# A thresholded attention with a leaky MoE layer behind it: the first periods rebuilt, and unread products on TensorE

## The chip, the cores and the metric

The kernel runs on one core of one Trainium2 chip. The metric is device time in microseconds. One core has five engines that run side by side, each through its own list of instructions in order: TensorE (PE in the profile, with its weight loads as PEld), VectorE (DVE), ScalarE (ACT), GpSimd (POOL) and SyncE (SP, which here only issues transfers). An engine waits where an instruction needs something that another engine or a transfer has not finished.

## The reference

```python
def _attn_ref(q, k, v, tau):                  # q, k, v: (8, 8, 576, 64), tau = 0.02
    scale = 1.0 / np.sqrt(q.shape[-1])
    scores = scale * np.matmul(q, k.transpose(0, 1, 3, 2))
    thresh = np.max(scores, axis=-1, keepdims=True) - tau
    scores = np.where(scores >= thresh, scores, -1000000000.0)
    scores = scores - np.max(scores, axis=-1, keepdims=True)
    attn = np.exp(scores)
    attn = attn / (np.sum(attn, axis=-1, keepdims=True) + 1e-09)
    return np.matmul(attn, v)

def _moe_ref(x, w_in, w_out):                 # x: (4608, 512), w_in: (512, 2048), w_out: (2048, 512)
    h = x @ w_in
    g = np.maximum(0.01 * h, h)
    return g @ w_out
# the output is _moe_ref of the attention's output, heads side by side
```

The threshold makes a score's last digits matter: a score just above or just below it is kept or lost. So the kernel computes scores from q and k split into two fp16 halves each (a high one and what is left, a low one), with three products out of the four.

## The kernel before

**Periods.** The attention is cut into 72 periods: 9 for each of the 8 batches. A period has one pair of heads and 256 of the first 512 queries as two chunks of 128 (8 periods: two blocks of queries by four pairs), or the last 64 queries of all eight heads (the ninth, `st.tail`). The main loop over `n` writes out by hand what each engine gets in iteration `n`, and each engine keeps to that order:

- `scores`: 24 matmuls (48 in a tail period) into one PSUM tile `sc` of five banks. Its four regions are (chunk, head). Head 0 and head 1 use different rows of the array, and the list alternates between them. Since regions (1, 0) and (1, 1) share bank 2, head 1's part of it waits for an empty instruction of GpSimd (`signal`, a `nop` at L246) that follows head 0's part.
- `copies`: VectorE copies the four regions to SBUF with the sign turned and the scale applied, taking the row minimum on the way (L257), and works out the threshold `th` (L259).
- `widen(n-1)` and `turn_w(n-1)`: GpSimd spreads the reciprocals of the row sums (L292), and SP issues the transposing transfer `wT <- w` (L297).
- `low_at`, `loads_at`, `turns_at`, `pool_at`: work for coming batches, put down by iteration. GpSimd splits q and k into halves (L144, L150, L154) and casts v (L105, L110); SP loads; TensorE turns the halves (`turn`, L183) and ScalarE copies them out (L186, L190). GpSimd also issues the loads of the MoE weights, `w_in` (L114) and `w_out` (L117), which cast on the way.
- ScalarE: `exp_plain` on three regions (L271), `exp_steep` on the fourth (a steep Prelu at L276 and an exponential at L277).
- MoE: two rounds, each with one unit of `layer1` (16 or 32 matmuls, L349, then L351 on ScalarE) and two units of `layer2` (4 matmuls each, L362), taken from the queues `l1q` and `l2q`. A group of four periods makes 256 tokens and gives 8 units of layer 1 and 16 of layer 2.
- `pv(n-2)`: weights times v (L309), two periods behind (`PV_LAG`), and after it VectorE's `evacuate` (L329, L321), which multiplies by the reciprocal and writes the MoE's input `x`.
- `weights` (L282), three on VectorE, with the row sums, and `finish`: the reciprocal (L288) of the four row sums, which needs ScalarE's steep region too.

PSUM tiles with the tag "h" (turned halves, `pv`, layer 1) share two buffers; layer 2 has one of its own ("o"). Before the loop, the first keys of batch 0 are split and turned: pair 0's k and q, then the k tails, on ScalarE and VectorE (`split_now`, L164 and L165), the others on GpSimd.

Of the kernel before, what the change touches and what calls it, by code (L numbers as in the profile page):

```python
# [9 lines left out]
FP32 = mybir.dt.float32  # L10
FP16 = mybir.dt.float16
# [3 lines left out]
PV_LAG = 2  # L15
# [21 lines left out]
def kernel(  # L37
# [24 lines left out]
    ident = sb.tile([128, 128], FP16, name="ident")  # L62
    minus_tau = sb.tile([128, 1], FP32, name="minus_tau")
# [18 lines left out]
    def load_tails(b, which):  # L82
        t = sb.tile([128, 2, 2, 64], FP32, tag="rawt", bufs=2, name="rawt")
        src = SRC[which][b, :, MAIN:S, :].rearrange("(u sh) p d -> u p sh d", u=2)
        for u in range(2):
            nc.sync.dma_start(out=t[ds(64 * u, 64), :, :, :].rearrange("p s h d -> p (s h) d"), in_=src[u])
        tails[b, which] = t
# [35 lines left out]
    turned, halves, scaled = {}, {}, {}  # L123
# [44 lines left out]
    def turn(key, copy=None):  # L168
        copy = copy or nc.scalar.copy
        b, p, which = key  # L170
        dst, half = turned_of(b, which), halves.pop(key)
        n = 2 if p == "t" else 4
        c0 = 0 if which == "q" else 64
        if p == "t":
            c0 = MAIN if which == "q" else 0
            tp = ps.tile([128, 2, 2, 2, 64], FP16, tag="h", bufs=2, name="tp")
        else:
            tp = ps.tile([128, 2, 4, 128], FP16, tag="h", bufs=2, name="tp")
        for x in range(2):
            for t in range(n):  # L180
                for h in range(2):
                    o = tp[ds(64 * h, 64), x, :, t, :] if p == "t" else tp[ds(64 * h, 64), x, t, :]
                    nc.tensor.transpose(o, half[:, x, t, h, :], ident[:, :])  # L183
        if p == "t":
            for x in range(2):
                copy(out=dst[:, x, :, ds(c0, 64)], in_=tp[:, x, :, :, :].rearrange("d u s p -> d (u s) p"))  # L186
            if which == "k":
                nc.gpsimd.tensor_copy(out=dst[:, :, :, 576:640], in_=dst[:, :, :, 0:64])
        else:
            copy(out=dst[:, :, p, ds(c0, 512)], in_=tp[:, :, :, :].rearrange("d x t p -> d x (t p)"))  # L190
# [38 lines left out]

    def scores(st):  # L230

        (a00, a01), (b01, b00) = pieces(0, 0), pieces(0, 1)
        (a11, a12), (b12, b11) = pieces(1, 0), pieces(1, 1)
        todo = [[(1, a12), (0, a00), (0, a01), (1, a11)], [(0, b00), (0, b01), (1, b11), (1, b12)]]
        todo = [[(c, x, i) for c, x in row for i in range(3)] for row in todo]
        at_, signal = [0, 0], None
        while todo[0] or todo[1]:
            h = 1 if not todo[0] or (todo[1] and at_[1] < at_[0]) else 0
            c, x, i = todo[h].pop(0)
            at_[h] += x[1]  # L240
            for mm in product(st, c, h, x, i):
                if (h, x) == (1, b12) and i == 0:
                    tc.add_manual_dep(mm.ins, signal.ins.name, BEHIND, reason="the row halves share a bank")
                last = mm
            if (h, x) == (0, a12) and i == 2:
                signal = nc.gpsimd.nop()  # L246
                tc.add_manual_dep(signal.ins, last.ins.name, BEHIND, reason="the row halves share a bank")

    TILES = ((0, 1), (0, 0), (1, 0), (1, 1))

    def copies(st):
        st.mn = sb.tile([128, 4], FP32, tag="mn", bufs=2, name="mn")
        st.th = sb.tile([128, 4], FP32, tag="th", bufs=2, name="th")
        st.s = {}
        for n, t in enumerate(TILES):
            st.s[t] = sb.tile([128, 576], FP32, tag=f"s{n}", bufs=1, name="s")
            nc.vector.tensor_scalar(out=st.s[t][:, :], in0=sc[:, ds(PLACE[t], 576)], scalar1=-1.0 / UNIT, scalar2=None,  # L257
                                    op0=AX.mult, op1=AX.min, accum_out=st.mn[:, n : n + 1])
        nc.vector.tensor_scalar(out=st.th[:, :], in0=st.mn[:, :], scalar1=1.0, scalar2=tau_f, op0=AX.mult, op1=AX.add)  # L259
        st.w = sb.tile([128, 2, 10, 128], FP16, tag="w", bufs=3, name="w")  # L260
        st.sum = sb.tile([128, 2, 2], FP32, tag="sum", bufs=3, name="sum")
        st.e = {}
# [23 lines left out]
    def finish(st):  # L286
        rec = sb.tile([128, 2, 2], FP32, tag="rec", bufs=2, name="rec")
        nc.vector.reciprocal(out=rec[:, :, :], in_=st.sum[:, :, :])  # L288
        st.rec = rec
# [24 lines left out]
    def evacuate(st, n):  # L314
# [17 lines left out]
        if done:  # L332
            nu = 8 if xg.tokens == 256 else 4
            l1q.extend((xg, u, nu, n + 1) for u in range(nu))
# [50 lines left out]
    def at(d, n, f):  # L385
        d.setdefault(n, []).append(f)
# [10 lines left out]
    def split_at(n, key):  # L397
        if key[0]:
            at(pool_at, n - 2, lambda key=key: split_scale(key))
            at(pool_at, n - 2, lambda key=key: split_high(key))  # L400
            at(low_at, n - 1, lambda key=key: split_low(key))
        else:
            at(pool_at, n - 1, lambda key=key: split_pool(key))
        at(turns_at, n, lambda key=key: turn(key))

    for b in range(1, B):
        base = PERB * (b - 1)
        for i, (s, w_) in enumerate(((0, "k"), (0, "q"), (1, "k"), (1, "q"))):
            at(loads_at, base + ((-2, -1, 2, 3)[i] if b > 1 else (1, 1, 3, 3)[i]),
               lambda b=b, s=s, w_=w_: load_main(b, s, w_))  # L410
        for i, w_ in enumerate("kq"):
            at(loads_at, base + ((-1, 5)[i] if b > 1 else (2, 4)[i]), lambda b=b, w_=w_: load_tails(b, w_))
        for i, key in enumerate(units(b)):
            split_at(base + 2 + 8 * i // 10 if b > 1 else base + 4 + i // 2, key)
    for b in range(B):
        base = PERB * (b - 1)
        if b:
            for s in range(2):
                at(loads_at, base + 5 + s, lambda b=b, s=s: load_v(b, s))
            at(loads_at, base + 6, lambda b=b: load_vtails(b))  # L420
        for p in range(NP):
            at(pool_at, base + 8 + p if b else 2 + p // 2, lambda b=b, p=p: cast_v(b, p))
        at(pool_at, base + 8 if b else 2, lambda b=b: cast_vtails(b))


    masks.make_identity(nc, ident[:, :])
    nc.gpsimd.memset(minus_tau[:, :], -tau_f)
    load_pair(0, "k", nc.sync)
    load_pair(0, "q", nc.scalar)
    load_tails(0, "k")  # L430
    load_pair(1, "q", nc.scalar)
    load_pair(1, "k", nc.sync)
# [11 lines left out]
    for i in range(4):  # L444
        load_w(i)
        at(pool_at, 3 + i, lambda i=i: load_w(4 + i))

    first = units(0)
    for key in first[:3]:
        split_now(key)  # L450
    turn(first[0])
    turn(first[1], nc.vector.tensor_copy)
    turn(first[2])
    for i, key in enumerate(first[3:]):
        if i < 2:
            split_pool(key)
            at(turns_at, 0, lambda key=key: turn(key))
        else:
            split_at((0, 0, 1, 1, 2, 2, 3)[i], key)
# [3 lines left out]
    while n < N + PV_LAG or l1q or l2q or stores:  # L463
        st = periods[n] if n < N else None
        if st:
            scores(st)
            copies(st)
        if 1 <= n <= N:
            widen(periods[n - 1])
            turn_w(periods[n - 1])  # L470
        for f in low_at.get(n, []):
            f()
        for f in loads_at.get(n, []):
            f()
        while stores:
            store()
        for f in turns_at.get(n, []):
            f()
        for f in pool_at.get(n, []):
            f()  # L480
        if st:
            exp_plain(st, 0)
        for half in range(2):
            if l1q and l1q[0][3] <= n:
                layer1()
            for _ in range(2):
                if l2q:
                    layer2()
            if st:
                if half == 0:  # L490
                    exp_plain(st, 1)
                    exp_plain(st, 2)
                else:
                    exp_steep(st, 3)
        if n >= PV_LAG and n - PV_LAG < N:
            pv(periods[n - PV_LAG])
        if st:
            weights(st, 0)
            weights(st, 1)
        if n >= PV_LAG and n - PV_LAG < N:  # L500
            evacuate(periods[n - PV_LAG], n)
        if st:
            weights(st, 2)
            finish(st)
        n += 1
# [33 lines left out]
```

## Time and profile before

| | us |
|---|---|
| median of 3 runs | 527.36 |
| the runs | 525.57, 527.36, 527.87 |
| the profiled execution's own time | 526.85 |
| its span, first to last instruction | 525.1 |
| PE busy | 472.8 (90%) |
| DVE busy | 435.1 (83%) |
| ACT busy | 422.3 (80%) |
| POOL busy | 256.3 (49%) |

Some 1.75 us of the profiled execution lie outside its span, and it is 0.5 us under the median. The first copy of period 0 starts at 16.04 us of the span, that of period 9 at 86.40, that of period 71, the last one, at 483.34. So the first nine periods take 70.4 us, 7.8 each, and the 62 after them 396.9 us, 6.40 each. What follows period 71 is the rest of the MoE work on TensorE.

### The profile page before, as it was taken

How to read it: one execution, taken by the hardware profiler on the slowest of the kernel's cores; microseconds unless marked ns; L12 is line 12 of the kernel's file. 1: busy time of each engine (PE TensorE's matmuls, PEld its weight loads, DVE VectorE, ACT ScalarE, POOL GpSimd, SP SyncE). 2: the span in 40 equal slices, each digit the busy share in tenths (PEclk: the TensorE clock that was granted, in tenths of full speed). 3: DMA queues.
4: the chain of work that ended last, by engine and by line, in shares of the span. 5: the costliest groups of instructions: out<-in, count | busy, mean ns of one | idle time of the engine just before them, and what ended most of it. 6: DMA issues, size and time to landing. Idle time of an engine off the chain costs nothing. (4 is left out here: it accounts for less than half of the span.)

```text
span 525.1 us, 18850 instructions
## 1 busy us (share of the span) xinstructions
PE 472.8 (90%) x7744; PEld 372.1 (71%) x7744; DVE 435.1 (83%) x1231; ACT 422.3 (80%) x714; POOL 256.3 (49%) x410
## 2 busy tenths in 40 slices
PE   4666768998989999999999999999999999999995
PEld 3444556776777777777777777777777777777783
DVE  1778868999899999999899989999899989999300
ACT  3567678888989998898989998898989998778541
POOL 5889953655375645654384636563385531100000
PEclk9999689999999999999999999999999999999999
DMA  8978999588988699978998699789988796666511
GB/s 204 241 178 175 201 199 209 112 171 195 205 179 183 123 225 227 173 146 203 215 171 176 170 207 215 160 130 225 201 155 202 158 192 144 122 102 151 133 42 61
DMA packets 230806, 90.34 MB, mean 172 GB/s; under 512 B 201024, under 2 KB 227648, under 8 KB 230720
## 3 DMA queue, kind: packets, MB, share of 16 engines
q1 hardware_dynamic: 227488, 84.43, 76.7%
q0 software_dynamic: 2688, 4.19, 4.7%
q8 instruction: 60, 0.98, 0.8%
q10 hardware_dynamic: 544, 0.52, 0.3%
q14 instruction: 26, 0.21, 0.1%
HBM read 36.70 MB, written 9.44 MB: 88 GB/s over the span
## 5 line engine op out<-in xcount | busy, mean ns | idle before, releaser
L257 DVE TENSOR_SCALAR_CACHE_REDUCE s<-sc 128x576 f32<-128x576 f32 x288 | 199.0, 748 | 12.0 <-PE sc L227 11.5
L282 DVE SCALAR_TENSOR_TENSOR w<-s,th,e 128x576 f16<-128x576 f32 x216 | 184.2, 876 | 8.6 <-ACT e L271 1.1
L271 ACT ACTIVATE e<-s,mn 128x576 f16<-128x576 f32 x216 | 158.7, 773 | 20.2 <-DVE s L257 19.2
L362 PE MATMUL o<-wout,g 128*64 128x512 f16 x1152 | 148.9, 380 | 5.0 <-ACT osb L368 3.5
L349 PEld LDWEIGHTS <-win 128*64 128x64 f16 x2560 | 127.4, 110 | 29.2 <-issue 16.0
L349 PE MATMUL hp<-x,win 128*64 128x256 f16 x2048 | 134.4, 273 | 8.4 <-ACT kT L190 4.5
L227 PE MATMUL sc<-kT,qT 64*128 64x256 f16 (+7 forms) x1920 | 128.4, 298 | 12.0 <-DVE s L257 4.7
L292 POOL CAST w<-rec 128x256 f16<-128x256 f32 x72 | 28.7, 399 | 211.8 <-DVE rec L288 199.6
L227 PEld LDWEIGHTS <-qT 64*128 64x128 f16 (+1 forms) x1920 | 97.9, 101 | 35.0 <-issue 19.5
L351 ACT ACTIVATE g<-hp 128x512 f16<-128x512 f32 x144 | 84.6, 588 | 13.0 <-PE hp L349 13.0
L362 PEld LDWEIGHTS <-g 128*64 128x64 f16 x1152 | 69.6, 110 | 35.5 <-issue 8.5
L154 POOL TENSOR_TENSOR half<-scaled,half 128x512 f16<-128x512 f32 (+1 forms) x77 | 82.5, 1079 | 0.6
L309 PE MATMUL pv<-wT,v 128*64 128x256 f16 (+1 forms) x960 | 55.6, 251 | 12.2 <-DMA wT<-w 6.7
L309 PEld LDWEIGHTS <-v 128*64 128x64 f16 x960 | 44.6, 112 | 25.9 <-POOL v L105 5.3
L277 ACT ACTIVATE w<-s,minus_tau 128x576 f16<-128x576 f32 x72 | 55.8, 775 | 5.8
L276 ACT ACTIVATE s<-s,th 128x576 f32<-128x576 f32 x72 | 55.8, 775 | 0.9 <-DVE th L259 0.9
L183 PE MATMUL tp<-ident,half 128*64 128x128 f16 x1152 | 49.3, 236 | 8.0 <-ACT half L164 5.1
L150 POOL CAST half<-scaled 128x512 f16<-128x512 f32 (+1 forms) x77 | 52.1, 676 | 4.9
L183 PEld LDWEIGHTS <-half 128*64 128x64 f16 x1152 | 38.6, 119 | 22.1 <-issue 15.9
L190 ACT COPY kT<-tp 128x1024 f16<-128x1024 f16 x32 | 32.3, 1010 | 21.4 <-PE tp L183 21.4
L144 POOL TENSOR_SCALAR scaled<-raw 128x512 f32<-128x512 f32 x62 | 40.7, 657 | 10.2 <-DMA raw<-in_q_dram 8.3
L190 ACT COPY qT<-tp 128x1024 f16<-128x1024 f16 x31 | 31.4, 1014 | 14.1 <-PE tp L183 14.0
(32 smaller groups left out, 231.6 us busy)
## 6 DMA issues: line engine op xcount, KB each, us to landing
vraw<-in_v_dram SPq DMA_DIRECT2D x16, 512.0 KB, 5.0
out_dram<-osb SPq DMA_DIRECT2D x16, 512.0 KB, 3.7
raw<-in_k_dram SPq DMA_DIRECT2D x14, 512.0 KB, 4.7
raw<-in_q_dram SPq DMA_DIRECT2D x14, 512.0 KB, 4.4
win<-in_moe_w_in_dram POOLq DMA_DIRECT2D x4, 512.0 KB, 11.5
wout<-in_moe_w_out_dram POOLq DMA_DIRECT2D x4, 512.0 KB, 6.8
wT<-w SPq DMA_TRANSPOSE x72, 5.9
raw<-in_k_dram SPq DMA_DIRECT2D x4, 256.0 KB, 11.0
```

The costliest lines, as they stand in the source:

```text
L154: nc.gpsimd.tensor_tensor(out=halves[key][:, 1, 0:n, :, :], in0=scaled.pop(key)[:, 0:n, :, :], in1=halves[key][:, 0, 0:n, :, :], op=AX.sub ...
L183: nc.tensor.transpose(o, half[:, x, t, h, :], ident[:, :])
L190: copy(out=dst[:, :, p, ds(c0, 512)], in_=tp[:, :, :, :].rearrange("d x t p -> d x (t p)"))
L227: yield nc.tensor.matmul(out=o, lhsT=lhs, rhs=turned[st.b, "k"][rows, kx, pair, ds(key0, n)], start=(i == 0), stop=(i == 2), skip_group_ch ...
L257: nc.vector.tensor_scalar(out=st.s[t][:, :], in0=sc[:, ds(PLACE[t], 576)], scalar1=-1.0 / UNIT, scalar2=None, op0=AX.mult, op1=AX.min, acc ...
L271: nc.scalar.activation(out=st.e[t][:, :], in_=st.s[t][:, :], func=AF.Exp, bias=st.mn[:, n : n + 1], scale=-1.0)
L276: nc.scalar.activation(out=z, in_=z, func=AF.Prelu, bias=st.th[:, n : n + 1], scale=-1.0, alpha=1e20)
L282: nc.vector.scalar_tensor_tensor(out=w_of(st, t), in0=st.s[t][:, :], scalar=st.th[:, n : n + 1], in1=st.e[t][:, :], op0=AX.is_le, op1=AX.mult,
L309: nc.tensor.matmul(out=o, lhsT=v16[st.b % 2][:, 2 * c + u if st.tail else st.p, blk, :], rhs=rhs, start=(i == 0), stop=(i == 4), skip_grou ...
L349: nc.tensor.matmul(out=hp[ds(64 * c, 64), jj, :], lhsT=w_in16[:, i, ds(128 * j + 64 * c, 64)], rhs=g.x[:, i, :], start=(i == 0), stop=(i = ...
L351: nc.scalar.activation(out=g.g[:, ds(nj * u, nj), :], in_=hp[:, :, :], func=AF.Prelu, bias=0.0, scale=1.0, alpha=0.01)
L362: nc.tensor.matmul(out=g.o[ds(64 * c, 64), :], lhsT=g.g[:, j, ds(128 * m + 64 * c, 64)], rhs=w_out16[:, j, :], start=(j == 0), stop=(j == ...
```

## The change

The change touches two things, the first periods and the order inside every period.

In every period: the matmuls of the scores come in another order (head 0 begins with region (0, 0), head 1 with its part of the shared bank, and the waiting for the signal turns round). VectorE's first copy is that of region (0, 0), and it is put down as soon as the three pieces of it and of its neighbour in bank 1 are done; the matmuls that follow are told that it is not in their way. The reciprocal of period `n-1` moves from the end of period `n-1` to behind the first copy of period `n`. Of two turned keys in one iteration, the second is copied out behind `exp_plain(st, 0)` and no longer ahead of it.

In the first periods: the signal comes from ScalarE in periods 0 to 3. The k tails are loaded by ScalarE's queue, and are split, turned and copied out first (by VectorE), then pair 0's k, then its q. Pair 1 is split on ScalarE and VectorE too; pairs 2 and 3 on GpSimd, one iteration earlier than before. `w_in` is loaded in iterations 1 and 2, not ahead of the loop; `w_out` in 4 to 7, not 3 to 6; v of batch 0 is cast in iterations 1 and 2, not 2 and 3. In iterations 0 to 5 `pv` and `evacuate` come ahead of the MoE units, and a group that is done there may start its MoE in the same iteration. In iterations 0 to 4 twelve pairs of matmuls on a zero tile (`idle`, six ahead of `pv` and six behind) write a PSUM tile that nobody reads.

```diff
     def load_tails(b, which, eng=None):
...
-            nc.sync.dma_start(out=t[ds(64 * u, 64), :, :, :].rearrange("p s h d -> p (s h) d"), in_=src[u])
+            (eng or nc.sync).dma_start(out=t[ds(64 * u, 64), :, :, :].rearrange("p s h d -> p (s h) d"), in_=src[u])
...
+    TILES = ((0, 0), (0, 1), (1, 0), (1, 1))
...
-        todo = [[(1, a12), (0, a00), (0, a01), (1, a11)], [(0, b00), (0, b01), (1, b11), (1, b12)]]
+        todo = [[(0, a00), (0, a01), (1, a11), (1, a12)], [(1, b12), (1, b11), (0, b01), (0, b00)]]
...
             for mm in product(st, c, h, x, i):
-                if (h, x) == (1, b12) and i == 0:
+                if first is not None:
+                    tc.declare_no_dep(mm.ins, first.ins, reason="other banks")
+                if (h, x) == (0, a12) and i == 0:
                     tc.add_manual_dep(mm.ins, signal.ins.name, BEHIND, reason="the row halves share a bank")
                 last = mm
-            if (h, x) == (0, a12) and i == 2:
-                signal = nc.gpsimd.nop()
+            if (h, x) == (1, b12) and i == 2:
+                signal = (nc.scalar if st.n < 4 else nc.gpsimd).nop()
                 tc.add_manual_dep(signal.ins, last.ins.name, BEHIND, reason="the row halves share a bank")
-    TILES = ((0, 1), (0, 0), (1, 0), (1, 1))
...
+            if (h, x) == (0, a11) and i == 2:
+                first = copy_min(st, 0)
+    def copies(st, before):
+        if before:
+            recip(before)
+        copy_min(st, 1)
+        copy_min(st, 2)
+        copy_min(st, 3)
...
     load_pair(0, "k", nc.sync)
     load_pair(0, "q", nc.scalar)
-    load_tails(0, "k")
+    load_tails(0, "k", nc.scalar)
+    load_pair(1, "k", nc.sync)
     load_pair(1, "q", nc.scalar)
-    load_pair(1, "k", nc.sync)
...
+    first = units(0)
+    for key in (first[2], first[0], first[1]):
+        split_now(key)
+        turn(key)
+        take(key, None if key == first[0] else nc.vector.tensor_copy)
+    for key in first[3:5]:
+        split_now(key)
+    for key in first[5:7]:
+        split_pool(key)
+    for i, key in enumerate(first[3:9]):
+        at(turns_at, i // 2, key)
+    for key in first[7:9]:
+        at(pool_at, 0, lambda key=key: split_pool(key))
     for i in range(4):
-        load_w(i)
-        at(pool_at, 3 + i, lambda i=i: load_w(4 + i))
...
+        at(pool_at, 1 + i // 2, lambda i=i: load_w(i))
+        at(pool_at, 4 + i, lambda i=i: load_w(4 + i))
+    at(pool_at, 1, lambda: cast_vtails(0))
+    for p in range(NP):
+        at(pool_at, 1 + p // 2, lambda p=p: cast_v(0, p))
+    at(pool_at, 2, lambda: split_pool(first[9]))
+    at(turns_at, 3, first[9])
...
+    def idle(k):
+        for i in range(k):
+            for c in range(2):
+                nc.tensor.matmul(out=spare[ds(64 * c, 64), 0:256], lhsT=ident[:, ds(64 * c, 64)], rhs=blank[:, :],
+                                 start=True, stop=True, skip_group_check=True)
...
+        early = n < 6
...
+        keys = turns_at.get(n, [])
+        for key in keys:
+            turn(key)
+        for key in keys[:1]:
+            take(key)
+        if st:
+            exp_plain(st, 0)
+        for key in keys[1:]:
+            take(key)
...
+        if early:
+            if n < 5:
+                idle(6)
+            pv_of(n, n)()
+            if n < 5:
+                idle(6)
...
-        if n >= PV_LAG and n - PV_LAG < N:
-            pv(periods[n - PV_LAG])
+        x = (lambda: None) if early else pv_of(n, n + 1)
...
-            finish(st)
```

`pv_of(n, ready)` issues `pv(n-2)` and gives back its `evacuate`; called with a second pair of brackets it issues both at once. `take` is the second half of the old `turn`: the copying out of a turned key.

## The prediction

> **What bounds the kernel now.** I read the page's slices first, then the busy time by stage, the waits of the two stages, and the timeline of one settled period.
>
> ```profile
> PE   4666768998989999999999999999999999999995
> DVE  1778868999899999999899989999899989999300
> PEclk9999689999999999999999999999999999999999
> ```
> The first seven slices of PE (13.1 us each) stand at 4 to 8, then it is full; the clock has its one dip there.
>
> ```profile
> 16.00:41.00 25.00, 17.23 (x180) 12.16 (x180) 20.35 (x49) 16.37 (x24) 21.20 (x30) 1.00 0.78 194
> 86.40:435.00 348.60, 335.02 (x5735) 265.77 (x5732) 323.33 (x919) 311.35 (x526) 188.30 (x300) 1.00 0.87 180
> ```
> Busy time by stage (stretch; PE, PEld, DVE, ACT, POOL; clock, DMA share, GB/s). Settled, PE is busy 335.0 of 348.6 us and DVE 323.3: both are nearly the bound, and PE leaves 13.6 us to gain.
>
> ```profile
> PE pv L309 <- DMA wT<-w: 6.2, 2, 3.4
> PE pv L309 <- POOL v L105: 4.8, 2, 4.3
> PE sc L227 <- POOLq L246: 3.5, 3, 2.3
> DVE s L257 <- PE sc L227: 11.5, 4, 7.8
> ...
> PE hp L349 <- ACT kT L190: 6.4, 11, 0.7
> DVE rec L288 <- ACT w L277: 11.0, 24, 0.9
> ```
> The waits of 0 to 91 us (first four) and of 91 to 490 us: total, times, longest. At first PE waits for transposed weights, cast v and the signal. Later DVE's largest wait is the reciprocal's for ScalarE; PE's is for a copied kT.
>
> ```profile
> 91.60 0.80 DVE L282 SCALAR_TENSOR_TENSOR w<-s,th,e 128x576 f16<-128x576 f32 x1
> 92.33 0.08 DVE L282 DVE_READ_ACCUMULATOR w<-s,th,e 128x1 f32 x1
> 92.54 0.18 DVE L288 RECIPROCAL rec<-sum 128x4 f32<-128x4 f32 x1
> 92.64 0.73 DVE L257 TENSOR_SCALAR_CACHE_REDUCE s<-sc 128x576 f32<-128x576 f32 x1
> ```
> From the last weights' end (92.33) to the next copy 0.31 us pass, though the reciprocal itself moves its successor by 0.10.
>
> By first copies, periods 0 to 8 last 6.96, 7.61, 10.49, 6.60, 6.56, 7.62, 7.53, 10.01 and 6.98 us: 70.36.
>
> **The change part by part.** *The start.* The tails go first, so all waits for them: their loads landed at 6.38 and 6.71. ScalarE's table load (1.28) now stands behind them in its list, where before it ran at 1.80, and `take` of k stands ahead of the split of q. From the landing: table 1.28; tails split 0.34 and 0.49, turned 0.35, copied by DVE 0.45 (from its 0.68 for four times the width); k's low halves 0.72, turned 0.6, copied 0.99; q split 0.67, low 0.40, turned 0.55, copied 0.68; three quarters of the cold scores (3.06) 2.3. Together 9.8: first copy at 16.5 from a landing at 6.7. The tails' packets now share with SP's k loads; 7.6 would give 17.4. I take 17.0, **+1.0**.
>
> *Periods 0 to 4.* ScalarE's loop: 5.5 from the first take to the steep region's sum (24.00 to 29.49), then signal, last scores 0.3, a turned half 0.5 and hand-offs 0.3: 6.6 with a warm PE, 7.3 cold (scores 3.06 against 1.65, sixteen transposes 0.95 against 0.47). The signal on ScalarE stands behind its steep region, so it is ScalarE's period that counts, and idle products (12 pairs of 256 columns; 16 of `hp` take 0.87, so 1.3 us) lie in PE's wait. They could cost 0, or 2.6 cold once. Granted clock by stretch:
>
> ```profile
> 38.50:41.90 3.40, 3.40 (x36) 2.62 (x34) 1.74 (x7) 0.23 (x1) 3.32 (x5) 1.00 0.17 35
> 48.80:52.20 3.40, 1.36 (x19) 1.01 (x18) 3.26 (x10) 3.15 (x5) 3.34 (x5) 0.99 1.04 149
> 52.20:55.60 3.40, 2.24 (x29) 1.53 (x29) 3.27 (x11) 1.80 (x5) 3.12 (x5) 0.50 1.32 164
> 69.30:72.70 3.40, 1.98 (x32) 1.66 (x31) 3.25 (x11) 3.40 (x5) 2.27 (x4) 1.00 1.32 145
> ```
> After a full stretch scores take 1.65 (43.95); a stretch with 1.36 busy is followed by half clock, and one with 1.98 (69.30) is not; 2.24 in a cold one does not bring it back. Ahead of 41.9 no change is on record, but scores take 3.06, so PE was cold. With idle products, iteration 0 has 3.1 + 1.9 + 2.6 us in a row, then some 4.5 of 6.6: warm from about 19 us. The Trainium skill ("TensorE: Matmul & The Clock Gate", Part 1) has a clock at half until about 3.4 us of steady work, and at half again after such a gap; by it the loop is the 6.6 too, and the stretches above agree.
>
> Period 0: 6.95, still partly cold. Period 1: 6.7, DVE's products stretched by GpSimd (1.16 for 0.82). In period 2 the wait for v (4.35 on PE) goes: its casts are queued one iteration earlier, behind two `w_in` issues of 0.6.
>
> What is late next is `wT`, since `w_in` is issued right behind `widen(0)` and `widen(1)`. Landings before: four `w_in` at 10.85, 13.71, 16.69, 19.55, 2.9 apart, and meanwhile SP's 256 KB loads at 11.21, 16.84, 19.95; once `w_in` was done, at 21.04 and 21.71. So SP's queue has about a quarter of its speed beside it. `wT` alone lands in 4.9, of which 3 are work; beside two `w_in` (5.8) it has 1.5 done, then 1.5 more: 9.2. wT(0), issued at 24.3, lands at 33.5, `pv(0)` takes 0.7, and VectorE, which now has the evacuation ahead of its weights and queues them and the next copies behind it, is there at 32.8: 1.5 lost, 8.1 in period 2. wT(1), issued at 30.7 behind 2.9 us of batch 1's loads and beside two more `w_in`, lands at 42.9; VectorE is there at 40.5, shifted by 1.5: 3.1 lost, 9.6 in period 3. Ends: 0 (as wT(0) before, 5.0) and 5.4 each (as wT(5) before, 12.8). The skill ("DMA: Bandwidth & Descriptors", Queues, rings and completion order) lets an engine take turns between queues packet by packet, so the larger packets win; that agrees with the quarter.
>
> Period 4: 6.5. GpSimd's signal stands behind its splits there, 0.6 late, which is hidden by the stall.
>
> *Periods 5 to 8.* MoE begins in 5 instead of 6, so ScalarE has two `g` (0.59) between the exponentials, the first behind the evacuation: 7.6. Then 6.8. `w_out` now comes behind GpSimd's low halves, some 2 us after `wT` was issued and no longer just ahead of it:
>
> ```profile
> 61.38 0.82 POOL L117 DMA_DIRECT2D wout<-in_moe_w_out_dram  x1
> 62.21 0.41 POOL L292 CAST w<-rec 128x256 f16<-128x256 f32 x1
> ```
> That `wT` landed at 75.47, and PE waited 3.36 for it. I keep 0.9: period 7 takes 7.5, period 8 6.7.
>
> Sum: 6.95 + 6.7 + 8.1 + 9.6 + 6.5 + 7.6 + 6.8 + 7.5 + 6.7 = 66.45, **-3.9**.
>
> *Periods 9 to 71.* VectorE gains 0.31 - 0.10 = 0.2 a period and most of 11.0. But PE's work is 6.23 a period: scores 1.60, turns 0.48, layer 1 1.75, layer 2 1.75, `pv` 0.65. Over 54 periods to 435 that is 336, and 6.4 (kT, in iterations with two turns, where nothing changes) stays: at most 5.7 to gain. Against it, the reciprocal is one copy (0.7) later, and with it `widen` and `wT`; its slack to `pv` is mostly 2 to 5 us, but 0.04, 0.95, 1.03 and 0.88 where v loads lie ahead: about 1.5. Taking the second key behind an exponential is covered: 0.67 + 2 x 0.95 end as layer 1 and 2 (1.75) and the first copy do. I take **-1.5**. The last eight have no turns, VectorE binds at 5.94 to 6.12, and 0.2 each is **-1.5**. From 490 us PE is full in an unchanged order: 0.
>
> Sum: +1.0 - 3.9 - 1.5 - 1.5 = -5.9. 525.1 becomes 519.2, the execution's 526.85 becomes **521.0**, against a median of 527.36 (measurement tells apart about 0.5%, 2.6 us).
>
> **The rivals.**
> - *Transfers hide after all.* For: before, `w_in` started with the queue full, now half of it. No loss to `wT` (-4.6), the early landing (-0.5), all of PE's 5.7 (-4.2): 511.7.
> - *Idle products do not warm PE.* For: 2.24 of 3.4 left it cold. Four periods at 7.3 instead of 6.6: 523.8.
> - *VectorE gains, PE does not.* For: PE is at 96%. The settled gain is 0 (+3.0), and the later `wT` costs 0.5 at each of seven v loads (+3.5): 527.5, no change.
> - *Slower: the weights travel behind other loads all through the early stage.* Each evacuation of periods 0 to 3 now stands in VectorE's way; it decides once a `wT` needs over a period + 0.8, 7.4 us, from issue to landing. Before, three of the first seven did (9.15, 12.82, 8.07). At 12.8 the first and third lose 5.4 each, the others follow in the longer periods: 10.8 instead of 4.6 (+6.2). With wT(5) as before (+2.5) and the late landing at the start (+0.5): 530.2. Against: landings of 5.0 to 5.3 for the first three before.
>
> **How the numbers follow.** 521.0 has 0.45 (own range 516 to 525.5), 511.7 0.14, 523.8 0.10, 527.5 0.16, 530.2 0.15. Faster by over 0.5% is under 524.7: 0.45 + 0.14 + 0.10, less 0.03 for the forecast's upper edge, 0.66. Same: 0.16 + 0.03 = 0.19. Slower: 0.15. The range leaves out half of the first and of the last rival: 511 to 530.5.
>
> **What would show it.** First copy near 17.0; scores of period 1 near 1.65 us; PE or VectorE waiting for `wT` in periods 2 and 3, and not for v; period 9 near 83.5; settled periods 6.35 instead of 6.40; no wait of the reciprocal for ScalarE there. Wrong if period 9 starts before 77 or after 87, or if settled periods fall below 6.3, which would mean that VectorE, not PE, was the bound.

## The result, and the profile after

The changed kernel takes 546.02 us (median of four runs, 542.94 to 547.64) where the kernel before, run beside it, takes 526.74: a ratio of 1.0359 (95% interval 1.0302 to 1.0417). It is slower by 3.6%, well outside the range of 511 to 530.5. The profiled execution took 547.64 us and its span is 545.9, 20.8 more than before's 525.1. By first copies this is where it went:

| | before | predicted | after |
|---|---|---|---|
| first copy of period 0, at | 16.04 | 17.0 | 19.80 |
| period 1 | 7.61 | 6.7 | 5.70 |
| period 2 | 10.49 | 8.1 | **22.64** |
| period 3 | 6.60 | 9.6 | 6.63 |
| periods 0 and 4 to 7 | 38.68 | 35.35 | 36.64 |
| period 8 | 6.98 | 6.7 | **17.00** |
| periods 9 to 62 | 348.69 | 347.2 | 349.15 |
| periods 63 to 70 | 48.25 | 46.75 | 46.10 |
| from the first copy of period 71 on | 41.7 | 41.7 | 42.2 |

Two periods of 72 carry the loss: against the forecast, period 2 is 14.5 us too long and period 8 10.3, together 24.8 of the 25.0 us between 521.0 and 546.0. The page's slices of the kernel after, of 13.6 us each:

```profile
PE   1733667389799999999999999999999999999995
DVE  1861988299999999899999999999899999999300
PEclk9985999699999999999999999999999999999999
```

Two holes stand in them: slices 3 and 4 (27 to 55 us; VectorE down to 1, the clock to 5) and slice 8 (96 to 109 us; PE 3, VectorE 2). In the first, by busy time (stretch; PE, PEld, DVE, ACT, POOL; clock, DMA share, GB/s), with the settled stretch below it:

```profile
42.00:49.00 7.00, 0.00 (x0) 0.00 (x0) 0.00 (x0) 0.00 (x0) 0.00 (x0) 0.50 1.17 144
...
108.41:455.00 346.59, 331.32 (x5671) 260.39 (x5669) 330.80 (x912) 307.61 (x519) 196.48 (x300) 1.00 0.87 181
```

For seven microseconds no engine does anything, while the DMA engines are full and move 144 GB/s, less than the settled stretch does on the side. The waits of 0 to 113 us say for what:

```profile
PE pv L325 <- DMA wT<-w: 27.7, 4, 16.8
DVE x L345 <- PE pv L325: 25.8, 3, 16.0
...
POOL scaled L145 <- DMA raw<-in_k_dram: 16.4, 1, 16.4
```

Before, the first of these was 6.2 us and its longest 3.4. The wait for v, 4.8 before, is gone, as the change meant. The other two lines are the same stop further back: VectorE's evacuation waits for `pv`, and GpSimd for batch 1's k, which stands behind `wT` in SP's queue. The timeline names the transfer:

```profile
27.98 1.31 POOL L115 DMA_DIRECT2D win<-in_moe_w_in_dram  x2
28.07 10.79 SPq L313 DMA_TRANSPOSE wT<-w  x1
33.69 1.05 POOL L115 DMA_DIRECT2D win<-in_moe_w_in_dram  x2
...
50.49 1.28 PE L325 MATMUL pv<-wT,v 128*64 128x256 f16 x10 [16.76 <-DMA wT<-w]
51.81 0.42 DVE L345 TENSOR_TENSOR x<-pv,wT 128x256 f16<-128x256 f32 x1 [15.95 <-PE pv L325]
```

wT(0) is issued with two pieces of `w_in`, meets the other two at 33.69 before it is done, and lands at 50.36, 22.3 us after its issue instead of 5.0. In slice 8 it is wT(6), with `w_out`'s last piece 1.6 us behind it; it lands at 104.69, 19.0 us after its issue:

```profile
85.69 7.28 SPq L313 DMA_TRANSPOSE wT<-w  x1
87.27 0.82 POOL L118 DMA_DIRECT2D wout<-in_moe_w_out_dram  x1
...
104.73 1.28 PE L325 MATMUL pv<-wT,v 128*64 128x256 f16 x10 [8.26 <-DMA wT<-w]
```

The settled part did what the change is made for, and gained little. VectorE, from the last weights of one period on:

```profile
249.56 0.80 DVE L298 SCALAR_TENSOR_TENSOR w<-s,th,e 128x576 f16<-128x576 f32 x1
250.29 0.07 DVE L298 DVE_READ_ACCUMULATOR w<-s,th,e 128x1 f32 x1
250.29 0.74 DVE L266 TENSOR_SCALAR_CACHE_REDUCE s<-sc 128x576 f32<-128x576 f32 x1
...
250.97 0.17 DVE L304 RECIPROCAL rec<-sum 128x4 f32<-128x4 f32 x1
251.06 0.72 DVE L266 TENSOR_SCALAR_CACHE_REDUCE s<-sc 128x576 f32<-128x576 f32 x1
```

The next copy follows without a gap, and the reciprocal moves its successor by 0.09. From 113 to 512 us the reciprocal waits 0.2 us in all, where it was 11.0. PE's wait for a copied kT, 6.4 then, is left:

```profile
PE hp L365 <- ACT kT L196: 7.2, 11, 0.7
```

### The profile page after: what moved, and what is told of

Its sections match the earlier page's. It is cut to its first block, busy times and chain, and to the rows that moved or that the text cites. A ratio compares the mean times of both kernels' runs of the same rounds, so it can differ in the third digit from the quotient of the medians.

```text
span 545.9 us, 19167 instructions
## 1 busy us (share of the span) xinstructions
PE 471.1 (86%) x7864; PEld 368.4 (67%) x7864; DVE 448.1 (82%) x1237; ACT 423.0 (78%) x716; POOL 259.6 (48%) x405
## 4 chain that ended last, share of the span: by engine, by line
PE 57%; ACT 7%; issue 2%; DVE 2%; DMA 2%; POOL 0%; POOLq 0%; DVEq 0%
PE o L378 18%; PE hp L365 16%; PE sc L233 14%; PE pv L325 5%; PE tp L181 4%; ACT kT L196 3%; DMA wT<-w 2%; ACT e L287 1%; ACT osb L384 1%; ACT qT L196 1%; ACT g L367 1%; DVE s L266 1%; DVE w L298 0%; POOL scaled L145 0%; DVE th L276 0%
## 5 line engine op out<-in xcount | busy, mean ns | idle before, releaser
L266 DVE TENSOR_SCALAR_CACHE_REDUCE s<-sc 128x576 f32<-128x576 f32 x288 | 204.0, 745 | 5.5 <-PE sc L233 2.4
L298 DVE SCALAR_TENSOR_TENSOR w<-s,th,e 128x576 f16<-128x576 f32 x216 | 191.3, 906 | 10.7 <-ACT e L287 3.5
L233 PE MATMUL sc<-kT,qT 64*128 64x384 f16 (+7 forms) x1920 | 123.8, 289 | 11.6 <-POOLq L259 6.2
L233 PEld LDWEIGHTS <-qT 64*128 64x128 f16 (+1 forms) x1920 | 91.8, 98 | 36.8 <-issue 13.7
L155 POOL TENSOR_TENSOR half<-scaled,half 128x512 f16<-128x512 f32 (+1 forms) x75 | 79.4, 1067 | 0.4
L151 POOL CAST half<-scaled 128x512 f16<-128x512 f32 (+1 forms) x75 | 56.2, 749 | 7.8 <-PE tp L181 3.2
L181 PE MATMUL tp<-ident,half 128*64 128x128 f16 x1152 | 46.6, 225 | 13.5 <-ACT half L165 10.9
L145 POOL TENSOR_SCALAR scaled<-raw 128x512 f32<-128x512 f32 x60 | 43.4, 723 | 27.1 <-DMA raw<-in_k_dram 16.4
L181 PEld LDWEIGHTS <-half 128*64 128x64 f16 x1152 | 35.4, 111 | 27.6 <-issue 12.8
L345 DVE TENSOR_TENSOR x<-pv,wT 128x256 f16<-128x256 f32 x64 | 26.9, 420 | 32.4 <-PE pv L325 31.8
```

The costliest lines, as they stand in the source:

```text
L151: nc.gpsimd.tensor_copy(out=halves[key][:, 0, 0:n, :, :], in_=scaled[key][:, 0:n, :, :])
L155: nc.gpsimd.tensor_tensor(out=halves[key][:, 1, 0:n, :, :], in0=scaled.pop(key)[:, 0:n, :, :], in1=halves[key][:, 0, 0:n, :, :], op=AX.sub ...
L233: yield nc.tensor.matmul(out=o, lhsT=lhs, rhs=turned[st.b, "k"][rows, kx, pair, ds(key0, n)], start=(i == 0), stop=(i == 2), skip_group_ch ...
L266: return nc.vector.tensor_scalar(out=st.s[TILES[n]][:, :], in0=sc[:, ds(PLACE[TILES[n]], 576)], scalar1=-1.0 / UNIT, scalar2=None, op0=AX. ...
L298: nc.vector.scalar_tensor_tensor(out=w_of(st, t), in0=st.s[t][:, :], scalar=st.th[:, n : n + 1], in1=st.e[t][:, :], op0=AX.is_le, op1=AX.mult,
```

## The experiments

Theory A: casting loads of the weights (`w_in`, later `w_out`) that are on the way together with a transposing transfer starve it. Theory B: the new order, with `pv` and the evacuation ahead of MoE and of the weights, turns any late `wT` into a stop. Where no number of runs is given, a kernel ran once; before, beside it, took 524.52 us for the first four, and a median of 530.23 and 528.0 for the single runs further down (packets and SP's queue; one piece and the last piece).

### Which part of the change it is

**w_in ahead of the loop**, as before; all else as in the change:

```diff
+    for i in range(4):
+        load_w(i)
+
     first = units(0)
...
-        at(pool_at, 1 + i // 2, lambda i=i: load_w(i))
```

> The changed kernel with the four w_in loads issued ahead of the loop, where they stood before the change; all else as changed. Theory A (w_in's packets starve the transposing transfers of periods 0 and 1): the first transfer lands within 6 us of its issue, period 2 falls from 22.6 to about 6.5 us, the first copy comes later again by up to 1 us because the loads of k and q share with w_in, the stall of period 8 (17.0) stays; time about 531 (16 off 546). Theory B (pv and evacuation ahead of the MoE units make any wait a stop of all engines): period 2 stays above 12 us, time above 538.

524.61 us, level with before. wT(0) landed 6.7 us after its issue and period 2 took 6.98. So this one move is worth some 21 us, 15.7 of them in period 2. Period 8 fell to 8.59 as well, though `w_out` stayed where the change has it; that was not expected (the time was to be 531), and no run explains it.

**All weights ahead**, `w_out` between GpSimd's first splits and in iteration 0:

> The changed kernel with all eight weight loads issued between GpSimd's splits ahead of period 1, so that none is beside a transposing transfer but the last w_out. Theory A: both stalls go, period 2 and period 8 last about 6.5 and 7 us, time about 521 to 523 (15.5 and 10 off 546, and 2 back for GpSimd's issue time ahead of the first splits). Theory B: the stall of period 8 belongs to the tail's order and stays at 12 or more, time above 530.

528.18 us, not 521 to 523. Period 8 took 6.90, but the last piece of `w_out` (issued at 28.25, landed at 37.73) and what is left of the two ahead of it now lie beside wT(0), which landed after 11.1, and period 2 took 12.48. The loss follows the casting load to whichever transfer it meets.

**PV late**: `pv` and the evacuation behind the MoE units in all iterations, the loads as in the change:

> The changed kernel with pv and its evacuation behind the MoE units in every iteration, as before the change (the twelve idle pairs of periods 0 to 4 stay, in one piece). Theory A: the transposed weights of period 0 still land some 20 us after their issue, so the wait is only met a little later in iteration 2: time 541 to 547. Theory B: the wait shrinks by what VectorE can do ahead of it, two weights or 1.6 us in each iteration and more by not stopping ScalarE: period 2 under 14 us, time under 538.

542.23 us, period 2 took 26.38, and wT(0) 27.0 from issue to landing. VectorE no longer waits ahead of its weights, and nothing is gained in period 2: theory B falls. Period 8, though, took 6.85, with `w_out` where the change has it and wT(6) landing after 9.5.

**The kernel before, with w_in alone moved** to iterations 1 and 2:

> The kernel before the change, with nothing but the four w_in loads moved into iterations 1 and 2, right behind widen. Theory A: the first transposing transfer lands 15 to 22 us after its issue instead of 5.0, one period of 0 to 3 lasts over 18 us, time 12 to 16 us above the kernel before, less 1 to 2 us that the early loads gain by having the queues to themselves: 538 to 541. Theory B: VectorE has its weights ahead of the evacuation here, so no more than 4 us are lost: under 532.

536.43 us: one move in the old kernel costs 12 us. wT(0) landed after 13.7, a little less than the 15 to 22 expected, and period 2 took 19.94. The stop has another look there:

```profile
PE pv L309 <- POOL v L105: 12.8, 1, 12.8
...
POOL scaled L144 <- DMA raw<-in_k_dram: 8.8, 1, 8.8
```

GpSimd waits for batch 1's k, which is queued on SP behind the slow `wT`, and the casts of v that `pv` needs stand behind that wait.

### What it is in the casting loads

**The same bytes in packets of 1 KB**, `w_in` in pieces of 512 columns instead of 128 rows:

```diff
-            nc.gpsimd.dma_start(out=w_in16[:, i, :], in_=moe_w_in[ts(i, 128), :])
+            nc.gpsimd.dma_start(out=w_in16[:, :, ts(i, 512)],
+                                in_=moe_w_in[:, ts(i, 512)].rearrange("(j p) f -> p j f", p=128))
```

> The changed kernel with w_in still loaded in iterations 1 and 2, but in four pieces of 512 columns instead of four of 128 rows: the same bytes in packets of 1 KB instead of 4 KB. Theory A1 (what starves the transposing transfer is the size of the packets that it takes turns with): wT(0) lands 10 to 13 us after its issue instead of 22.3, period 2 takes 10 to 13 us instead of 22.64, the time is 530 to 537. Rival A2 (any casting load beside a transposing transfer has this effect, whatever its packets): wT(0) lands 20 us or more after its issue, period 2 stays above 20, the time 543 to 549. Period 8 is to stay long by both (15 to 17 us), since w_out's packets were of 1 KB already and wT(6) landed 19.0 us after its issue beside them; if that is so, A1 is weakened by it.

540.72 us, wT(0) after 17.4, period 2 18.14, period 8 13.15: between the two, nearer to A2. With packets of 4 KB the same transfer took 22.3, 27.0 and 28.6 us in three kernels, so 17.4 may owe something to the packets, but a quarter of the size takes away a fifth to two fifths of the time.

**The same packets on SP's own queue**: `w_in` ahead, and plain loads of the same number and size of packets behind `turn_w` in iterations 1 and 2:

```diff
+    def more(i):
+        nc.sync.dma_start(out=w_out16[:, ds(4 * i, 4), :].rearrange("p j f -> p (j f)").bitcast(FP32),
+                          in_=moe_w_in[ts(i, 128), 0:1024])
...
+            if n in (1, 2):
+                more(2 * n - 2)
+                more(2 * n - 1)
```

> The changed kernel with w_in issued ahead of the loop (as in the run of w_in ahead, 524.6 us), and four plain loads on SP right behind the transposing transfers of iterations 1 and 2, each with as many packets of 4096 B as one w_in piece, into w_out's place, which is overwritten later. Theory Q (it takes a second queue, a casting load on GpSimd's, to starve the transfer; bytes behind it in SP's own queue only come later): wT(0) lands 6 to 9 us after its issue, wT(1) up to 4 us later than without the loads, period 2 takes 6 to 9 us, the time is 525 to 531. Rival B (bytes and packets that are on the way at the same time do it, on any queue): wT(0) lands 13 us or more after its issue, period 2 takes over 14 us, the time is above 535.

```profile
28.03 3.20 SPq L313 DMA_TRANSPOSE wT<-w  x1
31.28 1.05 SPq L485 DMA_DIRECT2D wout<-in_moe_w_in_dram  x2
34.10 7.86 SPq L313 DMA_TRANSPOSE wT<-w  x1
```

530.42 us, level with before. wT(0) lands 6.6 us after its issue, as without the loads, and period 2 takes 6.31. wT(1), which has two loads ahead of it in the queue, comes later, 9.9 after its issue, and periods 3 and 4 take 9.95 and 11.88. That agrees with theory Q: behind the transfer in its own queue, the same bytes do it no harm. What of the casting load does the harm is not separated by this: that it is in another queue, that it casts, or that it is issued ahead of the transfer and not behind it. Plain loads in a second queue beside a `wT` were not tried.

**One piece beside each transfer**: two pieces of `w_in` ahead, one each in iterations 1 and 2:

> The changed kernel with two pieces of w_in issued ahead of the loop and one each in iterations 1 and 2, so that one piece instead of two is issued beside wT(0), and one beside wT(1). In proportion (17.4 us over the undisturbed 4.9 by four pieces, 4.4 each): wT(0) lands 9 to 11 us after its issue, period 2 takes 8 to 11 us, and wT(1) lands 9 to 11 after its. If the delay only jumps with several pieces on the way: wT(0) lands 5.5 to 7.5 us after its issue and period 2 takes 5.5 to 7. If any piece does the whole of it: 15 us or more, period 2 over 15. Period 8 as it will, by the w_out pieces, 8 to 17 us.

530.05 us. wT(0) landed after 12.2, period 2 took 12.77; wT(1) after 8.9. One piece costs wT(0) 7.3 us over the 4.9 of a `wT` alone, two and then two more cost 17.4 to 23.7 over it. That is somewhat above the proportional case, and neither of the other two. In the old kernel with `w_in` moved, though, two and then two cost only 8.8.

### Period 8 and w_out

**Only the last piece of w_out one iteration later:**

```diff
-        at(pool_at, 4 + i, lambda i=i: load_w(4 + i))
+        at(pool_at, 8 if i == 3 else 4 + i, lambda i=i: load_w(4 + i))
```

> The changed kernel with only the last piece of w_out in iteration 8 instead of 7. If that piece, issued 1.6 us behind wT(6), made period 8 long: wT(6) lands 6 to 9 us after its issue instead of 19.0, period 8 takes 6.5 to 8 us instead of 17.00, and wT(7) pays instead, 9 to 14 us; together the time is 535 to 543. If the third piece's remainder and the v loads made it: wT(6) still lands 13 us or more after its issue, period 8 takes over 12 us and the time is 543 to 550.

```profile
91.77 6.61 SPq L313 DMA_TRANSPOSE wT<-w  x1
99.17 0.82 POOL L118 DMA_DIRECT2D wout<-in_moe_w_out_dram  x1
99.25 5.66 SPq L313 DMA_TRANSPOSE wT<-w  x1
```

wT(6) landed 10.1 us after its issue instead of 19.0 and period 8 took 6.90 instead of 17.00; wT(7), beside the moved piece, took 13.7 instead of 16.2, and period 9 11.88 instead of 6.08. So without the piece behind wT(6) period 8 is not long, and the piece takes 5.8 of the 10.1 us along when it moves. It does not set the length alone: with it in its place, period 8 took 6.85 with PV late and 8.59 with `w_in` ahead. The time, 547.97, missed, because period 2, where nothing was changed, took 29.18 in this run.

The next kernels start from one with a **mended start**: loads and splits of the first k and q ahead of the tails, as before; the tails' copy on VectorE and the signal on ScalarE, as in the change; `w_in` issued on GpSimd once the first tails have landed.

```diff
-    load_tails(0, "k", nc.scalar)
+    load_tails(0, "k")
...
-    for key in (first[2], first[0], first[1]):
-        split_now(key)
-        turn(key)
-        take(key, None if key == first[0] else nc.vector.tensor_copy)
+    nc.gpsimd.tensor_copy(out=blank[:, 0:1], in_=tails[0, "k"][:, 0, 0, 0:1])
+    nc.gpsimd.memset(blank[:, :], 0.0)
+    for i in range(4):
+        load_w(i)
+    for key in first[:3]:
+        split_now(key)
+    for key in first[:3]:
+        turn(key)
+        take(key, None if key == first[0] else nc.vector.tensor_copy)
...
-        at(pool_at, 1 + i // 2, lambda i=i: load_w(i))
```

> The changed kernel with another start and w_in early: loads and splits of the first k and q ahead of the tails as before, only the tails' copy on VectorE and the signal on ScalarE as in the change; w_in issued on GpSimd as soon as the first tails have landed (about 7 us) instead of in iterations 1 and 2. From the rows of before: tails copied by 9.4, kT's copy on GpSimd by 10.1, three quarters of the cold scores 2.6: first copy at 12.5 to 14 instead of 19.80. wT(0) is issued at about 21, behind the last of the first batch's loads, and lands 7 to 10 us later; period 2 takes 6 to 9. Periods 0 to 8 then take 60 to 66, and the time is 515 to 521. If bytes that are still on the way at 21 us starve wT(0) as in the changed kernel (landing 15 us or more after its issue), period 2 takes 14 or more and the time is 523 to 530.

522.0 us, the median of four runs, ratio 0.9833 (0.9757 to 0.9909). The first copy is at 13.74, wT(0) lands after 6.4, and period 2 takes 6.71. Periods 0 to 8 take 67.6 and not 60 to 66: of that, 41.6 are periods 4 to 8, beside `w_out`.

**w_out in halves**, at the end of GpSimd's list, one each in iterations 2 to 7 and two in iteration 8:

> The kernel with the mended start, and w_out in eight casting loads of 256 rows instead of four of 512, one at the end of GpSimd's list in each of iterations 2 to 7 and two in iteration 8. Theory (a transposing transfer pays for the casting bytes that are on the way with it, so half the piece costs about half the delay, and issued at the end of the list it falls between two transfers): the transfers of iterations 4 to 8, which landed 9.3 to 12.3 us after their issue, land after 6 to 8.5; periods 4 to 9 take 41 to 45 us instead of 48.7, the ratio to before is 0.968 to 0.978 instead of 0.983. Rival (SP's own loads and GpSimd's late signal make these periods long, not w_out): periods 4 to 9 stay at 47 to 50 us and the ratio at 0.98 to 0.985.

525.56 us over ten runs, ratio 0.9974 (0.9939 to 1.0009): no gain. Two transfers with the last half issued 1.9 and 4.2 us ahead of them landed after 6.3 and 5.7; two with a half issued behind them, after 10.6 and 14.7. But with two halves 5.5 and 6.2 us ahead wT(8) took 12.1, so the place does not decide alone. Period 9 took 12.30, and periods 4 to 9 50.6 us.

**w_out earlier**, whole pieces at the end of the list in iterations 3 to 6:

> The kernel with the mended start, and w_out in its four pieces of 512 rows, but each at the end of GpSimd's list in iterations 3 to 6 instead of at the head of it in iterations 4 to 7: ahead of the next signal, of widen and of the transposing transfer instead of some 2 us behind it. My prediction put period 7's loss on that order alone. If the order decides: the transfers beside w_out land 6 to 8 us after their issue instead of 9.3 to 12.3, periods 4 to 9 take 43 to 46 us instead of 48.7. If the bytes decide whatever the order, they land after 9 to 13 and periods 4 to 9 take 47 us or more.

520.51 us over four runs, ratio 0.9882 (0.9851 to 0.9913). The transfers land after 5.6 to 12.0 and periods 4 to 9 take 47.9 against 48.7. Period 8 gets shorter (6.90 for 8.53), period 5 longer (12.13 for 10.84). The order alone does not decide; my prediction's reading of period 7 was wrong in that.

**w_out spaced**, on a kernel with PV late (below), in iterations 3, 5, 7 and 9, and that kernel unspaced again on the same chip:

> The kernel with the mended start and pv late, with the four w_out pieces at the head of GpSimd's list in iterations 3, 5, 7 and 9 instead of 4 to 7, so that no transposing transfer has parts of two pieces beside it. If two at once cost more than one after the other: the transfers land 6.5 to 9 us after their issue, periods 3 to 10 take 49 to 53 us instead of 57.7, the time is 4 to 8 us below that of the same kernel unspaced. If each piece costs its share wherever it is: periods 3 to 10 take 56 to 60 us, the time within 2 us.

> The kernel with the mended start and pv late, unchanged, to stand beside the spaced one on the same chip: ratio to before 0.982 to 0.99, periods 3 to 10 56 to 60 us.

Spaced, 517.11 us, ratio 0.9837 (0.9775 to 0.9898); unspaced, 521.56, ratio 0.9888 (0.9804 to 0.9973), four runs each. Periods 3 to 10 take 58.1 spaced and 61.8 unspaced, or 59.3 in the unspaced kernel's first run (the 57.7 of the expectation was added up wrongly). The longest landing falls from 13.2 to 10.8. That is at most a part of what I expected, and with intervals that overlap it stays open whether spacing gains anything.

### The other parts

**The settled part alone**, on the old start and early periods:

> The kernel before with only the part of the change that acts in the settled periods: the reciprocal behind the first copy instead of behind the last weights, the order of the score products and of the tiles, the first copy ahead of the last bank's products, the second key's copy behind the first exponential. Start, load times, early signal, PV ahead of MoE and idle products as before. My working: settled periods 9 to 71 in 395.3 instead of 396.9 as in the changed kernel, nothing else moves by over 1 us: 523.5 to 525.5 against 526.7 (-1.5 to -3). Rival (the settled gain needs the changed start, or is a gain of later periods that the early ones give back): 526 to 528.

524.04 us over four runs beside 530.23 for the kernel before, ratio 0.9886 (0.9831 to 0.9941): more than the 1.5 to 3 us expected. Against before's own profile, the trace shows 2.0 us (span 523.1 for 525.1). Periods 9 to 62 take 348.9, within 0.3 of both kernels; periods 63 to 70 take 46.10 instead of 48.25. The early part moves within itself by more than the 1 us allowed: the first copy comes at 12.19 instead of 16.04 and period 0 takes 10.04 instead of 6.96.

**Without idle products**, on the mended start:

> The kernel with the mended start without the products that nobody reads (idle products left out of iterations 0 to 4). If they keep PE warm in the early periods (my prediction): scores of periods 1 to 4 take 2 to 3.1 us instead of 1.65 to 1.85, each of those periods is 0.4 to 0.8 longer, 2 to 3 us in all. Rival (my second: they do not warm PE, or ScalarE and VectorE hide it): periods 1 to 4 stay within 0.3 us each, and the time within 1 us, or gets shorter by the products' own 1.3 us a period.

523.39 us over five runs, ratio 0.9943 (0.9922 to 0.9963). Scores of period 2 without idle products, and then of the same period in the kernel with the mended start, with them:

```profile
23.41 2.81 PE L233 MATMUL sc<-kT,qT 64*128 64x384 f16 x24 [2.56 <-DVE s L266]
```

```profile
23.63 1.32 PE L233 MATMUL sc<-kT,qT 64*128 64x384 f16 x19 [1.94 <-DVE s L266]
25.30 0.82 PE L233 MATMUL sc<-kT,qT 64*128 64x256 f16 x5 [0.35 <-ACTq L259]
```

So they warm PE: 2.14 us of work instead of 2.81, and 1.82 instead of 3.06 in period 4; over period 0 the granted clock is 1.00 with them and 0.74 without. But periods 1 to 4 take 26.5 us with and 26.9 without them: most of it lies in PE's waits. The difference to the mended start (522.0, on another chip) lies in period 8 (11.98 for 8.53), beside `w_out`.

**PV late**, on the mended start:

> The kernel with the mended start, with pv and the evacuation behind the MoE units in all iterations as in the kernel before (the idle products stay). Now that w_in is out of the way, this shows what PV ahead of MoE is worth by itself. My prediction gave it no gain of its own and named its danger: VectorE's evacuation ahead of the weights waits for wT. Expected: a wT landing 6 to 10 us after its issue is no longer waited for by VectorE ahead of the weights, periods 2 to 5 shorter by 0 to 4 us in all, layer 1 begins one iteration later and periods 5 to 8 shift; the time between -3 and +1 us of the mended start's. Rival (PV ahead is a gain, as the change means it): +1 to +4 us.

517.43 us over four runs, ratio 0.9852 (0.9810 to 0.9895), on another chip than the mended start's 522.0 (0.9833); the same kernel's second time was 521.56. Periods 0 to 8 take 65.9 and 68.1, against 67.6 with PV ahead. PV ahead of MoE is worth nothing that these runs can show.

## Why the prediction was wrong

**The step that failed** is in the part on periods 0 to 4: "beside two `w_in` (5.8) it has 1.5 done, then 1.5 more: 9.2". I had seen that SP's queue has about a quarter of its speed beside `w_in`, from plain 256 KB loads, and used it for a transposing transfer, with `w_in` at its full speed of 2.9 us a piece. Both ends were wrong. In the profile, of the queues that ran from 24 to 29 us before (wT(0) with no casting load beside it) and from 39 to 45 after (packets, MB, share of 16 engines):

```profile
q1 hardware_dynamic: 2855, 0.79, 83.5%
```

```profile
q1 hardware_dynamic: 572, 0.15, 61.9%
q0 software_dynamic: 158, 0.57, 53.2%
```

q1 is SP's queue, q0 GpSimd's. In the first view, a packet of SP's queue took 0.835 x 16 x 5 us / 2855 = 23 ns; beside `w_in`, 0.619 x 16 x 6 / 572 = 104 ns, and only 95 packets passed in a microsecond instead of 571. `w_in` itself moved 0.57 MB in 6 us, where a piece of 0.5 MB had landed every 2.9 us at the start of the kernel before. Both went slower than without the other, so wT(0) was still on its way at 33.69, when iteration 2 issued the other two pieces (0.09 of its 0.66 MB had moved from 28 to 34 us). I had put these beside wT(1) alone, though my own times had them meet: wT(1) issued at 30.7, wT(0) landed at 33.5. That a late wT(0) would stop VectorE in period 2 was right; its landing was mis-sized, 22.3 us after the issue where I had 9.2, and so VectorE's wait for it, 16 us where I had 1.5.

The Trainium skill ("DMA: Bandwidth & Descriptors", Queues, rings and completion order) has each DMA engine take turns between its queues, a packet at a time. By turns alone four pieces could put no more than their own time in wT(0)'s way: 8 packets to an engine and piece, 4 x 8 x 323 ns (0.532 x 16 x 6 / 158) = 10.3 us, so an estimated landing after 15.2. Three kernels show 22.3 to 28.6, which turns do not explain; the old kernel with `w_in` moved stayed under it, with 13.7.

**The other places.**
- *wT(1)* landed after 13.5 (I had 12.2) and cost VectorE 0.33 us, not 3.1: it was issued at 44.34, inside the stop, and most of its way lay there. Period 3 took 6.63, not 9.6.
- *Period 8* I had at 6.7. "I keep 0.9" priced the transfer that had been late before, wT(5), and left out wT(6), behind which the last piece lies. It cost 10.3. Moving that piece moved more than half of the stop, so the kind of step was right, and its place and size were wrong.
- *The start* is 19.80 instead of 17.0. The tails landed at 7.76, where I had 6.7 to 7.6, and the table load began at 7.84. From there I had 9.8 us, and it took 12.0; the largest difference is the split of q, 2.06 us from ScalarE's start to VectorE's last low half instead of 0.67 + 0.40, with VectorE's share stretched to 1.61 while GpSimd splits beside it. That the tails are split first, and loaded on ScalarE's queue, costs some 6 us: the mended start, which undoes both, has its first copy at 13.74, while `w_in` ahead alone left it at 19.80.
- *Period 1* took 5.70 instead of 6.7, and the clock came as predicted: granted in full from iteration 0 until the stop (1.00 from 20.5 to 37.4 us). What I had wrong is that it matters: the run without idle products shows cold scores in periods 1, 2 and 4 (2.81 to 3.06 us) and periods 1 to 4 only 0.4 us longer in all.
- *Period 4* took 7.47 instead of 6.5. GpSimd's signal was not hidden by a stall there, PE waited 1.83 us for it; but with `w_in` ahead PE waited 2.11 and period 4 took 6.44, so the cause stays open.
- *The settled part*: VectorE's gap went as worked out, and the last eight periods gained 2.15 (I had 1.5). In periods 9 to 62, where I had 1.5, nothing was gained (+0.5): there PE has 331 busy us of 347, and what the reciprocal frees on VectorE is not on its path. The first half of my third rival, "VectorE gains, PE does not", was right.

**The rivals.** The slower one, weights that travel behind other loads, has the right wait and, for wT(0), the right place; it did not have period 8. Its point of decision, 7.4 us, does not tell the stops from the rest: of the first eight transfers all but wT(2) needed more, from 7.6 to 22.3, and two made a stop. Its price of 5.4 us each came from the largest landing that the kernel before showed, 12.8, beside two pieces of `w_out` one after the other (issued at 61.38 and 68.59, landed at 71.65 and 75.75); nothing in that trace had four pieces beside one transfer, and I took the nearest row for the end of the scale. With a chance of 0.15 it was also held to be too unlikely: the change puts four pieces of `w_in` into two iterations whose transfers had run alone.

**What stays open.** Why the same neighbours cost so differently. wT(0) beside four pieces took 22.3, 27.0 and 28.6 us in three kernels, but 13.7 in the old kernel with `w_in` moved. wT(6), with `w_out`'s last piece 1.6 to 1.7 us behind it, took 19.0 here and 9.5 to 15.2 in eight other runs. Nor is a transfer beside `w_in` always that slow. SP's queue in the old kernel with `w_in` moved, from wT(0)'s issue to its landing (22.7 to 36.4 us), and in the kernel after from 34 to 39 us:

```profile
q1 hardware_dynamic: 2610, 0.67, 31.8%
```

```profile
q1 hardware_dynamic: 1191, 0.30, 50.6%
```

That is 0.318 x 16 x 13.7 / 2610 = 27 ns and 0.506 x 16 x 5 / 1191 = 34 ns a packet, with `w_in` on the way in both; the 104 ns came after. So `w_in` beside wT(0) makes the stop, as moving it away and moving it in both show, but it does not set its length alone. What within the DMA engines lets the rate fall was not found.

## What to carry to other kernels

Before a load is moved, list for each transfer that the engines wait for what else is on the way beside it; a load that seems free because nobody needs it yet is not free if it shares its time with a transfer that somebody does. Where the trace shows such a meeting for one or two pieces only, the price of four is not their multiple with a safe upper end: leave the range open upwards, or put the loads where no awaited transfer runs. Here that is the stretch ahead of the first transposing transfer: the start with k and q first, `w_in` early there, and either order of `pv` ran 1.1 to 1.7% below the kernel before, and the change as it was made 3.6% above it.

## What the hardware showed that I had not expected

A transposing transfer and a casting load together can move less than each does in other company: wT(0) beside `w_in` ran at 0.15 + 0.57 MB in 6 us, 120 GB/s, with the DMA engines' share above 1, while SP's queue around wT(0) before moved 157 GB/s from 24 to 29 us, landing included, and `w_in` beside plain loads at the start of the kernel before went with 253 GB/s in all (2.7 to 19.5 us). The share of busy time does not tell these apart (0.84 before, 1.15 in the slow stretch, 1.06 at the start); the time of a packet of SP's queue (23 against 104 ns) does in the stop, though the old kernel's late wT(0) shows only 27. And a stretch in which all five engines stand still, as from 42 to 49 us, also cools PE: the granted clock is 0.50 there and 0.61 from 49 to 56, so `pv(0)` takes 1.28 us where a warm one takes 0.7.
